# Causal attention and a squared-ReLU MLP on one core: product times v merged with the next pair's scores, and earlier ranks for the raw weights of the h stages

## The chip, the cores and the metric

The kernel runs on one core of a Trainium2 chip. The metric is the device time of one execution in microseconds (us), taken as the median over runs. Every engine (PE for matrix products, DVE, ACT and POOL for elementwise work, SP for issuing DMAs) works through its own instruction stream in order, and semaphores connect them.

## The reference, cut to what matters

```python
# q, k, v: (4, 12, 448, 64) float32; w_in: (768, 2048), w_out: (2048, 768), both float64
scores = (q @ k.T) / 8                        # per batch and head
scores = where(upper triangle, -1e9, scores)  # causal
attn = exp(scores - max); attn = attn / (sum + 1e-9)
x = (attn @ v) -> (1792, 768)                 # tokens by 12 heads * 64
h = maximum(x @ w_in, 0)
out = (h * h) @ w_out                         # (1792, 768) float32
```

## The kernel before

**Units of work.** Two heads of a batch form a pair: 24 pairs, numbered n = 0 to 23 in the code. Pairs 0 to 11 (batches 0 and 1) run at the start with two sets of buffers (`a` for even, `b` for odd n) and leave x in SBUF, split into two float32r parts. Pairs 13 to 24 of the count (n = 12 to 23) run later, one after the other in the order of the list `turns`, all in buffer set `a`, between the MLP matmuls of the first 896 tokens. Their results go to DRAM through `spill`, for the last part of the kernel.

**A pair** (function `attention`). The loads of q and k and every third time of v; two 32x32-block transposes on DVE; the scores (line 386: 28 float32 matmuls of 64x64 tiles for the seven chunks of 64 queries; n < 12 has them in two groups, n >= 12 in one); per chunk a mask-and-minimum on DVE (399) and an exp on ACT (403); the inverse of the sums (470, 471); seven normalisations on POOL or DVE (412); sixteen 128x128 transposes on PE in four banks (426), each bank copied to `pt` on ACT or DVE (434 or the helper at 311); then the product with v (446: 16 float32 matmuls with a 128x64 stationary tile) into one bank `av`; then x or the spill. In the spill of n >= 18 a DVE subtraction (513) reads `av` too.

**MLP.** The first 896 tokens go through four groups of 512 columns of d_ff. A group has an h stage (`h_unit`, lines 634 to 636: w_hi x_hi + w_hi x_lo + w_lo x_hi, six inner tiles, 448 columns) and an o stage (`o_unit`, 1010 to 1012, 384 columns). Its weights come as float64 words: `piece` loads 128 rows into one of three `raw` buffers (587), two ACT operations and three DVE operations (595, the helper at 314, 598) make float32 of them, and two more split it into float32r parts (helpers at 318 and 324). Six pieces of kind "i" serve an h stage, eight of kind "o" an o stage. The other 896 tokens go through seven products in place of eight (`h_pair`, `o_seven`), after about 398 us.

**What sets the order.** Nothing runs where it is written: `Plan.op` collects operations with a rank, what they read and write, and the time that they are reckoned to take; `Plan.emit` then puts them on the engines one at a time. Of all ready operations it takes the one that can start first by its own reckoning, and among equals the one of lower rank. An operation is one indivisible stretch of an engine's stream. `lag` delays the time from which it may be placed. A bank of PSUM is held through `Hold("ps", kind)`: eight banks, and for each kind a cap on how many are held at once (`mm` for MLP results, `sc` for scores, `pt` for transposes, `av`).

The ranks are written as times in us. Pair n < 12 has rank 8.6 n, and its q and k loads 14 less. The late pairs are spread evenly over the ranks of the four groups. A piece has a rank `at`; its load stands at `at - 12`, its ACT operations at `at - 4`, its DVE operations at `at - 2`, its split at `at`. For the first h stage `begin` is 10.0 and the other end is `start`, 12 * 8.6 + 4 = 107.2; for the later ones the two ends are those of the o stage before it.

```python
key = (w[1], o.rank)                              # start by the plan, then rank
groups = (ORDER[:3], ORDER[3:]) if n < NA else (ORDER,)
at = begin + (rank - begin) * (c + 0.5) / NP      # rank of piece c of an h stage
```

Of the kernel before, what the change touches and what calls it, by code (L numbers as in the profile page):

```python
# [9 lines left out]
F32 = mybir.dt.float32  # L10
# [7 lines left out]
PE, ACT, DVE, POOL, DMA, DMA2 = range(6)  # L18
# [147 lines left out]
def t_dve(n, fast=False):  # L166
    return n / 1920 + 0.15 if fast else n / 960 + 0.15
# [13 lines left out]
def t_dma(count, size):  # L181
    return count * (0.0084 + size * 0.0000488) / 16
# [3 lines left out]
def kernel(  # L186
# [21 lines left out]
    P = 128  # L208
# [3 lines left out]
    NP = H // 2  # L212
# [15 lines left out]
    CW = [QC * (c + 1) for c in range(NQ)]  # L228
# [4 lines left out]
    TURNED = [(c, kc) for kc in range(NK) for c in range(2 * kc, NQ)]  # L233
    TOFF = [P * next(i for i, t in enumerate(TURNED) if t[1] == kc) for kc in range(NK)]
    NV = 3
    NA = 2 * NP
# [4 lines left out]
    CB = NP // 2  # L241
# [17 lines left out]
    psum = ctx.enter_context(tc.tile_pool(name="psum", bufs=1, space=bass.MemoryType.PSUM))  # L259
    plan = Plan()  # L260

    def tiles(nm, n, shape, dtype, pool=const):
        return [pool.tile(shape, dtype, name=f"{nm}{i}") for i in range(n)]
# [18 lines left out]
    spare = [whole[:, i * S:(i + 1) * S].bitcast(F32) for i in range((2 * NRAW + NZ + NB) * PCW // S)]  # L282
# [10 lines left out]
        nc.gpsimd.memset(t[KLAST:, NK - 1], 0.0)  # L293
    plan.pool("v", v_t)
    plan.pool("mx", tiles("mx", 8, [P, 1], F32))
    plan.pool("ps", tiles("ps", 8, [P, 512], F32, psum), mm=2, sc=4, pt=2, av=1, st=5, os=7)

    make_identity(nc, ident[:, :P])
    nc.vector.tensor_copy(ident[:, P:], ident[:, :QC])
# [10 lines left out]
    def on_act(n, dst, src, psum=False, func=AF.Copy, more=0, **kw):  # L310
        return (ACT, t_act(n, psum, more), lambda: nc.scalar.activation(dst(), src(), func, **kw))  # L311

    def on_dve(n, dst, a, b, op, more=0.0):
        return (DVE, t_dve(n) + more, lambda: nc.vector.tensor_tensor(out=dst(), in0=a(), in1=b(), op=op))  # L314
# [17 lines left out]
                list(reads) + [(key, 0)], [(key, 1)], after, drop=drop)  # L332


    vs = {}

    def attention(s, n, at):

        b, hp = divmod(n, NP)
        nm = s.nm  # L340
        spare = (lambda us: us) if n >= NA else (lambda us: 0.0)
# [31 lines left out]
        def softmax(chunks, at):  # L373

            pss = {b: Hold("ps", "sc") for b in sorted({PLACE[c][0] for c in chunks})}

            def place(c):
                b, o = PLACE[c]
                return pss[b].t[:, o:o + CW[c]]

            def scores():
                for c in chunks:
                    for j in range(2):
                        mine = slice(j * D, (j + 1) * D)
                        h = j ^ (PLACE[c][0] & 1)
                        nc.tensor.matmul(  # L386
                            place(c)[h * QC:(h + 1) * QC], s.qt[mine, c * QC:(c + 1) * QC],
                            s.kt[mine, :CW[c]], start=True, stop=True, skip_group_check=True)
            holds = tuple(pss.values())
            plan.op(at, [(PE, 0.16 + sum(2 * CW[c] / 2400 + 0.01 for c in chunks), scores)],  # L390
                    [(nm, "qt"), (nm, "kt")], holds, take=holds,
                    clear=[(nm, "p", c) for c in chunks], lag=spare(0.6))
            for c in chunks:
                exponential(c, lambda c=c: place(c), pss[PLACE[c][0]], Hold("mx", "mx"), at)

# [41 lines left out]
        def times_v(av, at):  # L437

            first = 2 * (n % NV)

            def go():
                for kc in range(NK):
                    m = NQ - 2 * kc
                    p = s.pt[:, TOFF[kc]:TOFF[kc] + m * P].rearrange("p (c j i) -> p c j i", j=2, i=QC)
                    for j in range(2):
                        nc.tensor.matmul(  # L446
                            av.t[j * D:(j + 1) * D, kc * P:S], vr.t[:, kc, first + j], p[:, :, j],
                            start=kc == 0, stop=kc == NK - 1, skip_group_check=True,
                        )
            plan.op(at, [(PE, 0.2 + 4 * sum((S - kc * P) / 2400 for kc in range(NK)), go)],  # L450
                    [vr] + [(nm, "pt", i) for i in range(len(TURNED) // 4)], [av], take=av, drop=[vr],
                    lag=spare(1.0))

        for j in range(2):
            load_qk("k", k, s.k, j)
# [4 lines left out]
        vr = vs[n // NV]  # L460
# [13 lines left out]
        for c in range(NQ):  # L474
            normalise(c, keys, at)
        at += 2
        av = Hold("ps", "av")
        for i in range(len(TURNED) // 4):
            transposed_p(i, at)
        times_v(av, at + 1)  # L480
# [1 line left out]
        if n < NA:  # L482
            x = x_t[n]
            plan.op(at, [on_act(S, lambda: x[:, 0], lambda: av.t[:, :S], True)],
                    [av], [(("x", n), 0)])
            plan.op(at, [on_dve(S, lambda: x[:, 1], lambda: av.t[:, :S],
                                lambda: x[:, 0].bitcast(F32), ALU.subtract)],
                    [av, (("x", n), 0)], [(("x", n), 1)], drop=[av])
        else:
            spill(n - NA, av, at)  # L490

    xt_dram = nc.dram_tensor("xt_dram", (4, CB, P, S), F32, kind="Internal").ap()
# [2 lines left out]
    def spill(n, av, at):  # L495

        b, c = divmod(n, NP)
        gate, mark = list(last_sums), len(plan.ops)

        def result():  # L500
            return av.t[:, :S]

        def stored(h, place, key):
            plan.op(at, [(DMA, 0.5, lambda: nc.sync.dma_start(out=place, in_=h.t), t_dma(P, 4 * S))], [h], [key], drop=[h])

        def loaded(place, key):
            h = Hold("r", "xs")
            plan.op(at - 8, [(DMA, 0.5, lambda: nc.sync.dma_start(out=h.t, in_=place), t_dma(P, 4 * S))],
                    [key], [h], gate, take=h)
            return h  # L510

        def less(h, drop):
            plan.op(at, [(DVE, t_dve(S) + 0.05, lambda: nc.vector.tensor_tensor(
                out=h.t, in0=result(), in1=h.t, op=ALU.subtract))], [av], [h], drop=drop)

        def t_place(k):
            return xt_dram[k - 1, c % CB], ("xt", k, c % CB)
        second = b == 1
        if second and c < CB:
            h = loaded(x_dram[c], ("xd", c))  # L520
            less(h, [av])
            stored(h, *t_place(1))
        elif second:
            t1 = loaded(*t_place(1))
            x21 = loaded(x_dram[c], ("xd", c))
            x12 = loaded(x_dram[n - CB], ("xd", n - CB))
            less(t1, [av])
            plan.op(at, two_sources(S, lambda: x21.t, lambda: x21.t, lambda: t1.t, ALU.subtract),
                    [t1], [x21])
            plan.op(at, [(DVE, t_dve(S) + 0.05, lambda: nc.vector.tensor_tensor(  # L530
                out=x12.t, in0=x12.t, in1=result(), op=ALU.subtract))], [av], [x12], drop=[av])
            stored(t1, *t_place(2))
            stored(x12, *t_place(3))
            stored(x21, *t_place(4))
        xs = Hold("r", "xs")
        plan.op(at, [
            on_act(S, lambda: xs.t, result, True),
            (DVE, t_dve(S) + 0.05, lambda: nc.vector.tensor_copy(xs.t, result())),
        ], [av], [xs], take=xs, drop=[av])
        last_sums[:] = plan.ops[mark:]  # L540
        stored(xs, x_dram[n], ("xd", n))
# [507 lines left out]
    def group(gr, rank, step, begin):  # L1049

        for c in range(NP):
            at = begin + (rank - begin) * (c + 0.5) / NP
            piece(at, "i", gr, c, 0, ())
            if gr in (0, NG - 1):
                keep(at + 4, gr, c, swap)
        begin = rank
        if gr == 0:
            r = NP * PAIR + 16
            for f in range(GF):
                r = h_unit(f, 0, r, (start - r) / (GF - f) / NP)  # L1060
            for f in range(GF):
                rank = h_unit(f, 1, rank, H_US * step)
        else:
            for f in range(GF):
                for h in range(2):
                    rank = h_unit(f, h, rank, H_US * step)
        for i in range(2 * GF):
            at = begin + (rank - begin) * (i + 0.5) / 8
            piece(at, "o", gr, i % GF, i // GF, swap)
        begin = rank  # L1070
        for ch in range(2):
            for t in range(NT):
                rank = o_unit(gr, t, ch, rank, O_US * step, swap)
        return begin, rank

    rank, begin = start, 10.0
    rest = NG * (2 * GF * NP * H_US + 2 * NT * GF * O_US) - GF * NP * H_US
    for gr in range(NG):
        begin, rank = group(gr, rank, (rest + NA * 7.0) / rest, begin)
    mark = len(plan.ops)  # L1080
    turns = [NA + NP * b + CB * g + i for g in range(2) for b in range(2) for i in range(CB)]
    for i, n in enumerate(turns):
        attention(even, n, start + i * (rank - start - 42) / NA)

# [32 lines left out]
    for gr, u in stages:  # L1117
        last = gr == TURNS[-1]
        if u is None:
            W = o_parts(gr, rank - LEAD, rank + 42 * H_US - LEAD)  # L1120
            rank = o_last(W, rank, H_US) if last else o_seven(gr, W, rank, H_US)
        else:
            W = w_parts(gr, u, rank - LEAD, rank + 7 * CB * H_US - LEAD)
            rank = h_pair(gr, u, W, rank, H_US, last)
# [33 lines left out]
```

## Time and profile before

| | |
|---|---|
| median of 3 runs | 616.55 us (613.45 to 618.95) |
| the profiled execution: its own time | 616.22 us |
| its span in the trace | 614.5 us |
| busy share of the span | PE 96%, PE weight loads 83%, DVE 71%, ACT 58%, POOL 57% |
| mean granted PE clock | 0.994 of full speed |
| DMA | 120.01 MB, mean 195 GB/s |

The span is what the trace covers; the execution's own time has 1.7 us around it. The views used below are the page's busy times, busy times by stretch, waits by engine, the order of instructions in time, and the chain of work that ended last. In the order of instructions, columns are start, busy time from first start to last end, engine, line, operation, tiles, shape and count; matmuls overlap, so the time that one takes of PE is the distance from its start to the next start.

### The profile page before, as it was taken

The numbers are of one execution on the slowest core, as the hardware profiler recorded it, in microseconds if no ns is written. First come the engines' busy times: TensorE is split into PE (matmuls) and PEld (weight loads), VectorE is DVE, ScalarE is ACT, GpSimd is POOL, SyncE is SP. The second block draws the span as 40 slices with busy tenths as digits, with TensorE's granted clock in tenths as the row PEclk, the third lists the DMA queues.
The fourth block names the chain that finished last, engine by engine and source line by source line (L and its number), as shares of the span: only waits on it lengthen the run. The fifth ranks groups of instructions, "written<-read, shape, count | busy, mean of one in ns | idle before, by whom it ended". The sixth has DMA issues, their size and how long they took to land.

```text
span 614.5 us, 11390 instructions
## 1 busy us (share of the span) xinstructions
PE 589.3 (96%) x3714; PEld 511.0 (83%) x3714; DVE 436.9 (71%) x957; ACT 356.7 (58%) x878; POOL 352.5 (57%) x460
## 2 busy tenths in 40 slices
PE   3888999999999999999999999999999999999996
PEld 1555677789988988988998889989989999998995
DVE  4888776366786689785787326679994896399474
ACT  3787998657677845678555552247665534661220
POOL 2556575475589746788644764325865674478110
PEclk9899999999999999999999999999999999999999
DMA  9788856597888999998997477877958837963546
GB/s 140 159 199 146 175 99 132 106 308 243 249 222 256 293 264 220 275 265 277 245 279 249 163 209 220 266 219 194 228 103 198 224 71 161 221 105 95 149 76 106
DMA packets 203148, 120.01 MB, mean 195 GB/s; under 512 B 138960, under 2 KB 191056, under 8 KB 203088
## 3 DMA queue, kind: packets, MB, share of 16 engines
q1 hardware_dynamic: 181328, 108.01, 64.4%
q0 software_dynamic: 6912, 9.44, 10.2%
q10 hardware_dynamic: 14848, 1.84, 2.0%
q8 instruction: 29, 0.48, 0.3%
q14 instruction: 31, 0.25, 0.1%
HBM read 80.71 MB, written 38.54 MB: 194 GB/s over the span
## 4 chain that ended last, share of the span: by engine, by line
PE 81%; DVE 8%; DMA 5%; ACT 3%; issue 1%; POOL 1%; SPq 1%; DVEq 0%; ACTq 0%; POOLq 0%
PE ps L1010 7%; PE ps L634 7%; PE ps L1012 6%; PE ps L1011 6%; PE ps L636 6%; PE ps L635 6%; PE ps L426 6%; PE ps L446 6%; PE ps L386 5%; PE ps L937 5%; PE ps L939 5%; PE ps L938 5%; PE ps L815 4%; PE ps L811 4%; PE ps L813 4%; DVE g L314 2%
## 5 line engine op out<-in xcount | busy, mean ns | idle before, releaser
L412 POOL TENSOR_SCALAR ap<-ap,asm 128x128 f32<-128x128 f32 (+6 forms) x122 | 72.7, 615 | 52.3 <-DVE asm L471 41.6
L311 ACT ACTIVATE words<-words 128x384 f32<-128x384 f32 (+3 forms) x135 | 77.3, 596 | 32.9 <-DVE words L314 9.7
L399 DVE CUSTOM_DVE_ANT_0 ps<-ps,mask 128x448 f32<-128x448 f32 (+6 forms) x168 | 68.7, 444 | 28.2 <-PE ps L386 22.8
L1010 PE MATMUL ps<-wo,g 128*128 128x384 f32 x224 | 77.0, 344 | 0.0
L634 PE MATMUL ps<-x,wi 128*128 128x448 f32 x192 | 75.0, 391 | 0.6 <-ACT x L311 0.6
L1012 PE MATMUL ps<-wo,g 128*128 128x384 f32 x224 | 75.1, 335 | 0.0
L1011 PE MATMUL ps<-wo,g 128*128 128x384 f32 x224 | 75.0, 335 | 0.0
L636 PE MATMUL ps<-x,wi 128*128 128x448 f32 x192 | 70.9, 369 | 0.4 <-DVE wi L314 0.4
L635 PE MATMUL ps<-x,wi 128*128 128x448 f32 x192 | 70.7, 368 | 0.2 <-DVE x L314 0.2
L403 ACT ACTIVATE ap<-ps,mx 128x448 f32<-128x448 f32 (+6 forms) x126 | 58.7, 482 | 13.5 <-DVE mx L399 12.5
L937 PE MATMUL ps<-g,wi 128*128 128x448 f32 x162 | 59.5, 367 | 1.0 <-DVE sb L314 0.9
L311 ACT ACTIVATE r<-ps 128x448 f32<-128x448 f32 x59 | 32.1, 545 | 48.3 <-PE ps L815 15.8
L938 PE MATMUL ps<-g,wi 128*128 128x448 f32 x162 | 59.3, 366 | 0.0
L318 POOL TENSOR_TENSOR wi<-words,wi 128x384 fp32r<-128x384 f32 (+1 forms) x45 | 56.3, 1263 | 5.1 <-ACT wi L311 2.4
L939 PE MATMUL ps<-g,wi 128*128 128x448 f32 x162 | 59.2, 366 | 0.0
L324 POOL TENSOR_SCALAR wi<-words 128x384 fp32r<-128x384 f32 (+1 forms) x40 | 26.8, 672 | 47.4 <-DVE words L598 14.4
L811 PE MATMUL ps<-x,wi 128*128 128x448 f32 x141 | 51.8, 368 | 0.0
L813 PE MATMUL ps<-x,wi 128*128 128x448 f32 x141 | 51.7, 367 | 0.0
L815 PE MATMUL ps<-x,wi 128*128 128x448 f32 x141 | 51.7, 366 | 0.0
L314 DVE CUSTOM_DVE_ANT_0 words<-words 128x768 uint16<-128x768 uint16 (+1 forms) x56 | 45.7, 816 | 5.3 <-ACT words L311 1.9
L311 ACT ACTIVATE apt<-ps 128x512 f32<-128x512 f32 x70 | 38.4, 602 | 17.4 <-PE ps L426 17.4
L595 DVE TENSOR_SCALAR words<-words 128x384 int32<-128x384 int32 (+1 forms) x56 | 29.1, 521 | 21.5 <-ACT words L311 21.1
(138 smaller groups left out, 1476.1 us busy)
## 6 DMA issues: line engine op xcount, KB each, us to landing
words<-in_moe_w_in_dram SPq DMA_DIRECT2D x24, 512.0 KB, 5.3
words<-in_moe_w_out_dram SPq DMA_DIRECT2D x32, 384.0 KB, 4.2
wo_split<-wo SPq DMA_DIRECT2D x26, 384.0 KB, 4.8
wi<-wo_split SPq DMA_DIRECT2D x24, 384.0 KB, 4.5
wo_whole<-words SPq DMA_DIRECT2D x32, 192.0 KB, 4.0
wi_split<-wi SPq DMA_DIRECT2D x24, 256.0 KB, 4.0
v<-in_v_dram SPq DMA_DIRECT2D x24, 192.0 KB, 4.2
wi_whole<-words SPq DMA_DIRECT2D x18, 256.0 KB, 4.3
```

The costliest lines, as they stand in the source:

```text
L311: return (ACT, t_act(n, psum, more), lambda: nc.scalar.activation(dst(), src(), func, **kw))
L634: nc.tensor.matmul(o, w[:, 0], x[:, 0], start=c == 0, stop=False)
L635: nc.tensor.matmul(o, w[:, 0], x[:, 1], start=False, stop=False)
L636: nc.tensor.matmul(o, w[:, 1], x[:, 0], start=False, stop=c == NP - 1)
L811: nc.tensor.matmul(o, w.t[:, 0, c], x[:, 0], start=begin and c == 0, stop=False, skip_group_check=True)
L813: nc.tensor.matmul(o, w.t[:, 0, c], x[:, 1], start=False, stop=False, skip_group_check=True)
L937: nc.tensor.matmul(o, w.t[:, 0, d], g.t[:, 0], start=start, stop=False, skip_group_check=True)
L938: nc.tensor.matmul(o, w.t[:, 0, d], g.t[:, 1], start=False, stop=False, skip_group_check=True)
L939: nc.tensor.matmul(o, w.t[:, 1, d], g.t[:, 0], start=False, stop=stop, skip_group_check=True)
L1010: nc.tensor.matmul(res(), g[:, 0], w[:, 0], start=f == 0, stop=False)
L1011: nc.tensor.matmul(res(), g[:, 0], w[:, 1], start=False, stop=False)
L1012: nc.tensor.matmul(res(), g[:, 1], w[:, 0], start=False, stop=f == GF - 1)
```

## The change

The product with v of a late pair is no longer an operation of its own. For all late pairs but the last it is put on a list (`waiting`) with its bank, its reads, the hold on v and its spill; the next pair's scores operation takes it up: it issues the 16 product matmuls first and then its own 28 score matmuls, reads what both read, and takes five banks at once (four for scores, one for `av`, now of kind `sc`, whose cap goes from 4 to 5). The spill of the earlier pair is entered after it, at the rank of the next pair's scores plus 2. The lag of the joint operation is that of the scores, 0.6, where the product alone had 1.0. The last late pair keeps its own product and spill.

The second edit multiplies the span over which the six pieces of an h stage are ranked by 0.9, in all four groups, from the same beginning.

```diff
-    plan.pool("ps", tiles("ps", 8, [P, 512], F32, psum), mm=2, sc=4, pt=2, av=1, st=5, os=7)
+    plan.pool("ps", tiles("ps", 8, [P, 512], F32, psum), mm=2, sc=5, pt=2, av=1, st=5, os=7)
...
-    vs = {}
+    vs, waiting = {}, []
+    turns = [NA + NP * b + CB * g + i for g in range(2) for b in range(2) for i in range(CB)]
...
             def scores():
+                if before:
+                    before[0][1]()
                 for c in chunks:
...
-            holds = tuple(pss.values())
-            plan.op(at, [(PE, 0.16 + sum(2 * CW[c] / 2400 + 0.01 for c in chunks), scores)],
-                    [(nm, "qt"), (nm, "kt")], holds, take=holds,
+            holds, before = tuple(pss.values()), list(waiting)
+            waiting.clear()
+            more = [x for w in before for x in w[2]]
+            avs = tuple(w[0] for w in before)
+            plan.op(at, [(PE, 0.16 + 1.9 * len(before) + sum(2 * CW[c] / 2400 + 0.01 for c in chunks), scores)],
+                    [(nm, "qt"), (nm, "kt")] + more, holds + avs, take=holds + avs, drop=[w[3] for w in before],
                     clear=[(nm, "p", c) for c in chunks], lag=spare(0.6))
+            for w in before:
+                w[4](at + 2)
...
+            reads = [vr] + [(nm, "pt", i) for i in range(len(TURNED) // 4)]
+            if n in turns[:-1]:
+                waiting.append((av, go, reads, vr, lambda rank: spill(n - NA, av, rank)))
+                return
             plan.op(at, [(PE, 0.2 + 4 * sum((S - kc * P) / 2400 for kc in range(NK)), go)],
-                    [vr] + [(nm, "pt", i) for i in range(len(TURNED) // 4)], [av], take=av, drop=[vr],
-                    lag=spare(1.0))
+                    reads, [av], take=av, drop=[vr], lag=spare(1.0))
...
-        av = Hold("ps", "av")
+        av = Hold("ps", "sc" if n in turns[:-1] else "av")
...
-        else:
+        elif n == turns[-1]:
             spill(n - NA, av, at)
...
-            at = begin + (rank - begin) * (c + 0.5) / NP
+            at = begin + 0.9 * (rank - begin) * (c + 0.5) / NP
```

## Rows read from the trace of the kernel before

**Rows 1.** The page, busy time, share of the span and instructions by engine:
```profile
PE 589.3 (96%) x3714; PEld 511.0 (83%) x3714; DVE 436.9 (71%) x957; ACT 356.7 (58%) x878; POOL 352.5 (57%) x460
```
**Rows 2.** Busy times by stretch; the first line names the columns:
```profile
core 0: us, PE busy (x) PEld busy (x) DVE busy (x) ACT busy (x) POOL busy (x), PEclk, DMA share, GB/s
...
31.00:65.00 34.00, 28.95 (x259) 19.53 (x253) 27.57 (x87) 27.21 (x81) 18.97 (x31) 0.95 0.86 181
65.00:120.00 55.00, 53.90 (x464) 39.75 (x457) 38.16 (x130) 44.94 (x139) 31.00 (x55) 1.00 0.58 111
120.00:398.00 278.00, 278.00 (x1832) 247.41 (x1831) 190.33 (x422) 166.95 (x406) 182.67 (x216) 1.00 0.87 250
398.00:614.50 216.50, 210.08 (x1028) 192.14 (x1026) 161.25 (x244) 100.70 (x203) 107.89 (x128) 1.00 0.67 155
```
**Rows 3.** Order of PE's instructions, 152 to 159 us, separate operations:
```profile
152.18 0.34 PE L1012 MATMUL ps<-wo,g 128*128 128x384 f32 x1
152.44 1.95 PE L446 MATMUL ps<-apt,v 128*64 128x448 f32 x16
154.32 0.44 PE L1010 MATMUL ps<-wo,g 128*128 128x384 f32 x1
154.61 0.34 PE L1011 MATMUL ps<-wo,g 128*128 128x384 f32 x1
154.78 0.34 PE L1012 MATMUL ps<-wo,g 128*128 128x384 f32 x1
...
156.34 0.34 PE L1012 MATMUL ps<-wo,g 128*128 128x384 f32 x1
156.61 1.75 PE L386 MATMUL ps<-akt,aqt 64*64 64x448 f32 x28
158.29 0.44 PE L1010 MATMUL ps<-wo,g 128*128 128x384 f32 x1
158.57 0.34 PE L1011 MATMUL ps<-wo,g 128*128 128x384 f32 x1
```
**Rows 4.** Order of PE's instructions, 176 to 181 us, adjacent operations:
```profile
176.07 0.36 PE L636 MATMUL ps<-x,wi 128*128 128x448 f32 x1
176.36 1.95 PE L446 MATMUL ps<-apt,v 128*64 128x448 f32 x16
178.24 1.75 PE L386 MATMUL ps<-akt,aqt 64*64 64x448 f32 x28
179.92 0.47 PE L634 MATMUL ps<-x,wi 128*128 128x448 f32 x1
180.23 0.36 PE L635 MATMUL ps<-x,wi 128*128 128x448 f32 x1
180.43 0.36 PE L636 MATMUL ps<-x,wi 128*128 128x448 f32 x1
```
**Rows 5.** The chain that ended last, the other adjacent place (start, us):
```profile
283.41 1.88 PE ps L446 x16
285.29 1.66 PE ps L386 x20
```
**Rows 6.** Order of ACT's instructions, copies of transposes for the pair of rows 3:
```profile
149.54 1.09 ACT L311 ACTIVATE apt<-ps 128x512 f32<-128x512 f32 x2
```
**Rows 7.** PE's waits, 31 to 65 us (total, times, longest us):
```profile
PE ps L426 <- ACT ap L403: 2.5, 1, 2.5
PE ps L386 <- ACT bpt L311: 1.0, 1, 1.0
```
**Rows 8.** Order of ACT's instructions, 44 to 60 us (idle before, releaser):
```profile
44.28 0.68 ACT L311 ACTIVATE words<-words 128x512 f32<-128x512 f32 x1 [1.71 <-DMA words<-in_moe_w_in_dram]
...
59.20 1.22 ACT L311 ACTIVATE words<-words 128x512 f32<-128x512 f32 x2 [3.09 <-DMA words<-in_moe_w_in_dram]
```
**Rows 9.** Order of PE's instructions, scores at 45 us:
```profile
45.49 2.80 PE L386 MATMUL ps<-bkt,bqt 64*64 64x448 f32 x28 [1.02 <-ACT bpt L311]
```
**Rows 10.** PE's waits, 398 us to the end (total, times, longest us):
```profile
PE ps L937 <- DVE sb L314: 0.9, 1, 0.9
```

## The prediction before the run

> **What bounds the kernel now.** I read the page's busy times first: PE is busy 589.3 us of a 614.5 us span [rows 1], so at most some 25 us can come from PE waiting less; all else has to come from PE doing less or doing it faster. The busy times by stretch say where those 25 us lie [rows 2]. From 120 to 398 us, where all late pairs run, PE is busy for the whole 278.00 us at full clock: no wait there can be shortened, and only time that PE's own stream takes counts. After 398 us it is idle for 216.50 - 210.08 = 6.4 us; one wait of 0.9 us on DVE is the only one listed [rows 10], the rest is the tail after the last matmul. From 65 to 120 us it is idle for 1.1 us. From 31 to 65 us it is idle for 34.00 - 28.95 = 5.05 us and the granted clock is 0.95, not 1.00. What is left of the 25.2 us, 12.6 us, lies in the first 31 us. So the first edit has to be priced in a stretch bound by PE, and the second in the stretch from 31 to 65 us, the only one in which the order of weights meets idle PE.
>
> **The joined operation, PE's own time.** The order of PE's instructions shows what a burst of float32 matmuls costs beside its own matmuls. In the o stage one MLP matmul follows the other at 0.17 us (154.61 to 154.78). The last one before the product with v takes 152.18 to 152.44, 0.26 us; the first one after it takes 154.32 to 154.61, 0.29 us. The scores are the same: 156.34 to 156.61 is 0.27 us on the way in, 158.29 to 158.57 is 0.28 us on the way out [rows 3]. So going in costs 0.09 to 0.10 us and coming out 0.11 to 0.12 us, some 0.20 us for each excursion. The bursts take 154.32 - 152.44 = 1.88 us and 158.29 - 156.61 = 1.68 us. In one place the plan before already put the two side by side: the product takes 178.24 - 176.36 = 1.88 us, the scores 179.92 - 178.24 = 1.68 us, with one entry (0.29 against 0.20 us for an h matmul, 180.23 to 180.43) and one exit (0.31 us) for both [rows 4]. The joint therefore costs nothing that a start-to-start distance shows, and a merge saves one entry and one exit: 0.20 us.
>
> Eleven products are merged. Two already stand next to their scores [rows 4, 5] and save nothing. In the nine others MLP matmuls stand between, as in rows 3. That is 9 x 0.20 = 1.8 us, in a stretch with no PE idle time to swallow it. Bounds: nothing, if the plan scatters its transposes into as many more excursions, and 11 x 0.23 = 2.5 us.
>
> A rule speaks against the full amount. The Trainium skill, page "TensorEngine Tiling (Array Packing)", section "Tiling Modes", says that a change of tiling mode drains the engine. Product and scores have different tile shapes, so by that rule the joint would still pay one change, three in place of four, and an estimate by it is half of the saving, 0.9 us. Rows 4 speak for the full 1.8 us: a drain at the joint would have made one of the two bursts longer than when it stands alone.
>
> **The joined operation, what it waits for.** It now waits for the last pair's four copies of transposes as well as for q and k. In rows 3 the copies that ACT makes run from 149.54 us for 1.09 us [rows 6], so they end near 150.6 us; the joint operation would start where the scores now end less both bursts, 158.29 - 1.68 - 1.88 = 154.7 us. That is 4 us of cover, and the scores themselves end where they did. In the two adjacent places it starts where the product started before. I cost this wait at nothing; if the cover went, MLP matmuls queued behind on PE would wait, by some tenths of a us for each pair. The five banks: four are free because the last pair's exps are long done (its transposes could not have run otherwise), and the fifth because the spill of the pair before that is a whole pair older. PSUM adds no wait.
>
> **The spill.** It moves from just after the product to just after the next scores, in rows 3 some 2 us, elsewhere up to the distance between a product and the next scores. It issues one store for each pair and for the six pairs with n >= 18 loads and stores more, on SP's queue; the same number as before, all behind loads that have been there longer. Nothing before 398 us reads what it stores, except later spills a pair or more away. The last pair, whose end lets the last part's x tiles be loaded, keeps its own product and spill. The DVE subtraction waits in DVE's order for the joint operation as it did for the product; the next pair's masking stands ahead of it by rank. Cost: nothing, covered by a pair's length (178.24 to 156.61, 21.6 us) [rows 3, 4].
>
> **The weights of the late h stages.** Three of the four sixes are ordered while PE has no idle time [rows 2], so earlier pieces buy nothing there. They cost nothing either as long as PE stays full.
>
> **The weights of the first h stage.** The six ranks run from 18.1 to 99.1 before and from 17.3 to 90.2 after (10 + 97.2 (c + 0.5) / 6, with 0.9 on the second term). The piece c = 1 has its load moved from 22.3 to 19.9, past the loads of pair 4 (4 x 8.6 - 14 = 20.4), and c = 2 from 38.5 to 34.5, past those of pair 6 (37.6); the last two move by 7 and 9. In this stretch ACT stood in front of a conversion whose words had not landed, for 1.71 us and for 3.09 us [rows 8], with exps queued behind it; PE waited 2.5 us for an exp and 1.0 us behind a copy of ACT's [rows 7]. PE also loses speed: after the wait of 1.02 us the scores took 2.80 us against 1.75 us of the same burst at full clock [rows 9, 3], 1.05 us more. A clock of 0.95 over 34 us is 1.7 us of lost PE time [rows 2]. So the most that this edit can gain is 5.05 + 1.7 = 6.75 us. Its loss is bounded by the nearest event: one more landing wait of the longest kind, 3.09 us, and the slow scores behind it, 1.05 us, together 4.1 us. Between -6.75 and +4.1 us I take -1.0 us: weights that are ready earlier let PE place matmuls of the h stage in the 2.5 us wait, and the two products of one inner tile on two open banks are six matmuls of 0.20 us, 1.2 us; but the ACT and DVE work pulled forward is work in front of exps.
>
> **The sum.** -1.8 - 1.0 = -2.8 us on the profiled execution's 616.22 us (span 614.5 and 1.7 around it) gives 613.4 us. The median shown, 616.55 us, is 0.3 us higher, which gives 613.7; I say 613.5 us.
>
> **The rivals.**
> - Much of the idle time of the first stretch goes. For it: ACT's two landing waits are an accident of order, and order is what changes. Against: the loads remain the same and the DMA engines are 0.86 busy there [rows 2]. Half of 6.75 us and the merge give 616.2 - 3.4 - 1.8 = 611.0 us, all of it 607.7 us.
> - Slower: a conversion moved ahead of exps meets words that have not landed. Place: ACT's stream between 31 and 65 us. Price: 4.1 us for each event like the second of rows 8, less the merge's 1.8: 618.5 us for one, 622.6 us for two. It decides as soon as ACT reaches a piece's first conversion before its load lands with exps behind it that PE needs next, which is what rows 7 and 8 show once. For it: it has happened; against: loads move earlier along with conversions.
> - The merge doesn't save what it says, because the plan spends the freed time on extra excursions, or because the last part gives it back on its waits: 616.2 - 0 to 1.0 = 615 to 616.5 us. For it: after 398 us PE does have a wait on DVE [rows 10]. Against: DVE's work there starts from PE's results, so it moves along.
> - The joint drains as in the tiling rule: 0.9 + 1.0 gives 614.3 us. This lies within the forecast's own range.
>
> **How the numbers follow.** Forecast (612 to 615 us, the tiling rule's 614.3 within it, a tenth by itself): 0.50. Much of the idle time gone (607.7 to 612): 0.20. Nothing saved (615 to 617): 0.15. Slower (617 to 623 and a little over): 0.15. The range 609.5 to 618.0 us leaves out about 0.08 below and 0.10 above. What a measurement of this kernel can tell from no change is 1%, 6.2 us: faster means under 610.4 us, which only the better half of the first rival reaches, 0.14; slower means over 622.7 us, two landing waits or more, 0.06; the same, 0.80.
>
> **What the profile after would show.** The merge: eleven bursts of line 446 followed at once by line 386 between 120 and 398 us, no PE wait in that stretch, and MLP matmuls as many as before; the stretch from the first late scores to the end of the o stages shorter by about 1.8 us. The weights: PE idle and the clock between 31 and 65 us against 5.05 us and 0.95, and ACT's waits for words against 1.71 and 3.09 us. The forecast is wrong if a PE wait appears in front of a joint operation, if the joint shows a longer burst than 1.88 + 1.68 us, or if the first 120 us move by more than 3 us either way.

## The result: 0.55% slower, and the profile after

The changed kernel took 620.71 us (median of 16 runs, 618.47 to 624.32) against 618.25 us (16 runs, 613.45 to 620.77): ratio 1.0055, 95% interval 1.003 to 1.0079. The forecast was 613.5 us with a range up to 618.0. Of the runs of before that the forecast started from, the profiled one (616.22 us) lies 2 us below the median of all; the profiled execution of after (618.50 us) likewise. TensorE's granted clock, as the mean over a run, was 0.984 to 0.996 of full speed in the sixteen runs of after and 0.996 in the profiled one, so its trace shows the changed kernel at its best.

Busy times of after by stretch, columns as in [rows 2]:

```profile
31.00:65.00 34.00, 28.32 (x238) 18.57 (x236) 26.54 (x87) 26.39 (x80) 17.22 (x28) 0.95 0.78 161
65.00:120.00 55.00, 54.17 (x464) 40.70 (x459) 40.28 (x135) 45.70 (x139) 31.22 (x53) 1.00 0.59 120
120.00:398.00 278.00, 277.29 (x1834) 248.22 (x1834) 193.76 (x428) 168.67 (x407) 181.53 (x215) 1.00 0.88 252
398.00:616.70 218.70, 209.28 (x1021) 190.78 (x1019) 161.50 (x236) 102.02 (x204) 112.53 (x131) 1.00 0.65 151
```

Up to 398 us little has changed. After it PE is idle for 218.70 - 209.28 = 9.4 us where it was 6.4 us [rows 2]. The first matmul of the seven products starts at 396.75 us (398.04 before) and the last matmul of all at 611.12 us (608.77 before): the profiled execution was 1.3 us ahead when the last part began and 2.3 us behind when it ended.

The joint operation itself is what the rows of before said. Order of PE's instructions of after, 153 to 157 us (lines 454 and 389 are now the product with v and the scores):

```profile
153.06 0.34 PE L1023 MATMUL ps<-wo,g 128*128 128x384 f32 x1
153.33 1.95 PE L454 MATMUL ps<-apt,v 128*64 128x448 f32 x16
155.21 1.75 PE L389 MATMUL ps<-akt,aqt 64*64 64x448 f32 x28
156.89 0.44 PE L1021 MATMUL ps<-wo,g 128*128 128x384 f32 x1
157.17 0.34 PE L1022 MATMUL ps<-wo,g 128*128 128x384 f32 x1
```

One entry (0.27 us), 1.88 us, 1.68 us, one exit (0.28 us), against two of each in [rows 3]. No PE wait stands in front of any of the eleven joint operations. The waits of PE between 120 and 398 us are these two (total, times, longest), both elsewhere:

```profile
PE ps L1023 <- POOL g L318: 0.4, 1, 0.4
PE ps L434 <- POOL ap L420: 0.3, 1, 0.3
```

PE's waits from 396 us to the end, which answer to [rows 10]:

```profile
PE ps L948 <- DVE sb L314: 3.1, 2, 1.7
PE ps L822 <- DMA w<-wi_split: 0.6, 1, 0.6
PE ps L948 <- DVE sa L314: 0.5, 1, 0.5
```

The 0.9 us has become 3.1 us. The DVE additions that PE waits for (`sb`, a sum that empties a bank) stand behind one held subtraction; "held" means here that the profile shows an instruction as busy for far longer than others of its shape. DVE of after, in order of time:

```profile
549.01 1.50 DVE L314 TENSOR_TENSOR g<-r,g 128x448 fp32r<-128x448 f32 x1
550.43 5.85 DVE L314 TENSOR_TENSOR g<-f,g 128x448 fp32r<-128x448 f32 x1
556.20 0.61 DVE L314 TENSOR_TENSOR sb<-ps,sb 128x448 f32<-128x448 f32 x1
```

POOL of after in the same time:

```profile
550.59 1.30 POOL L318 TENSOR_TENSOR wi<-words,wi 128x384 fp32r<-128x384 f32 x1
551.58 0.84 POOL L324 TENSOR_SCALAR g<-r 128x448 fp32r<-128x448 f32 x1
552.11 1.28 POOL L318 TENSOR_TENSOR wi<-words,wi 128x384 fp32r<-128x384 f32 x1
553.10 1.26 POOL L318 TENSOR_TENSOR w<-words,w 128x384 fp32r<-128x384 f32 x1
554.07 1.26 POOL L318 TENSOR_TENSOR wi<-words,wi 128x384 fp32r<-128x384 f32 x1
555.06 0.74 POOL L324 TENSOR_SCALAR wi<-words 128x384 fp32r<-128x384 f32 x1
```

And PE, which resumes twice after it (in brackets: idle before, releaser):

```profile
556.87 0.47 PE L948 MATMUL ps<-g,wi 128*128 128x448 f32 x1 [1.38 <-DVE sb L314]
...
560.08 0.47 PE L948 MATMUL ps<-g,wi 128*128 128x448 f32 x1 [1.73 <-DVE sb L314]
```

A subtraction that takes 0.61 us elsewhere lasted 5.85 us: it began beside the first of six POOL instructions without a gap and ended at 556.28 us, 0.48 us after the last of them (555.06 + 0.74 = 555.80). In the kernel before, POOL had nothing to do in these microseconds (3.02 us of idle ahead of its copy) and the DVE subtraction before it ran at full speed. POOL, then DVE, of the kernel before:

```profile
553.33 0.97 POOL L324 TENSOR_SCALAR g<-r 128x448 fp32r<-128x448 f32 x1 [3.02 <-ACT r L311]
```

```profile
552.19 0.61 DVE L314 TENSOR_TENSOR g<-f,g 128x448 fp32r<-128x448 f32 x1
```

Holds as such are not new. The kernel before has one of 4.26 us a little later, beside three POOL additions in a row (563.39 to 567.04 us); no PE wait stands behind it [rows 10]:

```profile
563.20 4.26 DVE L314 TENSOR_TENSOR wi<-f,wi 128x384 fp32r<-128x384 f32 x1
```

Neither edit touches this code. Its order comes from the same plan: of the 1131 operations entered for the last part, 90 stand on another engine than before, and the order differs on every engine (counted in the two plans). Theory A was therefore that the edits do save time and that the plan's new order of the last part loses more; the rivals, that the merge (B) or the earlier weights (C) cost by themselves.

### The profile page after: what moved, and what is told of

Same layout as the page of the kernel before. It is cut to its first block, busy times and chain, and to the rows that moved or that the text cites. A ratio compares the mean times of both kernels' runs of the same rounds, so it can differ in the third digit from the quotient of the medians.

```text
span 616.7 us, 11388 instructions
## 1 busy us (share of the span) xinstructions
PE 588.2 (95%) x3714; PEld 510.6 (83%) x3714; DVE 441.7 (72%) x956; ACT 360.9 (59%) x882; POOL 354.6 (58%) x457
## 4 chain that ended last, share of the span: by engine, by line
PE 81%; DVE 6%; DMA 4%; ACT 3%; POOL 2%; issue 1%; SPq 1%; DVEq 0%; POOLq 0%; ACTq 0%
PE ps L1021 6%; PE ps L645 6%; PE ps L1023 6%; PE ps L1022 6%; PE ps L647 6%; PE ps L646 6%; PE ps L454 5%; PE ps L822 5%; PE ps L824 5%; PE ps L826 5%; PE ps L434 5%; PE ps L948 5%; PE ps L950 5%; PE ps L949 5%; PE ps L389 4%; DVE g L314 2%
## 5 line engine op out<-in xcount | busy, mean ns | idle before, releaser
L420 POOL TENSOR_SCALAR ap<-ap,asm 128x64 f32<-128x64 f32 (+6 forms) x122 | 74.9, 635 | 52.4 <-DVE asm L482 35.7
L311 ACT ACTIVATE words<-words 128x384 f32<-128x384 f32 (+3 forms) x130 | 75.1, 597 | 35.0 <-DVE words L314 11.8
L645 PE MATMUL ps<-x,wi 128*128 128x448 f32 x192 | 73.9, 385 | 0.0
L647 PE MATMUL ps<-x,wi 128*128 128x448 f32 x192 | 70.3, 366 | 0.4 <-DVE wi L314 0.4
L646 PE MATMUL ps<-x,wi 128*128 128x448 f32 x192 | 70.2, 366 | 0.0
L318 POOL TENSOR_TENSOR wi<-words,wi 128x384 fp32r<-128x384 f32 (+1 forms) x46 | 59.8, 1311 | 6.3 <-ACT wi L311 4.8
L948 PE MATMUL ps<-g,wi 128*128 128x448 f32 x153 | 56.2, 367 | 3.6 <-DVE sb L314 3.1
L824 PE MATMUL ps<-x,wi 128*128 128x448 f32 x153 | 56.2, 368 | 0.0
L822 PE MATMUL ps<-x,wi 128*128 128x448 f32 x153 | 56.1, 367 | 0.0
L826 PE MATMUL ps<-x,wi 128*128 128x448 f32 x153 | 56.0, 366 | 0.0
L949 PE MATMUL ps<-g,wi 128*128 128x448 f32 x153 | 55.9, 365 | 0.0
L950 PE MATMUL ps<-g,wi 128*128 128x448 f32 x153 | 55.9, 365 | 0.0
L314 DVE CUSTOM_DVE_ANT_0 words<-words 128x768 uint16<-128x768 uint16 (+1 forms) x56 | 41.3, 738 | 9.3 <-ACT words L311 6.5
L314 DVE TENSOR_TENSOR g<-r,g 128x448 fp32r<-128x448 f32 x43 | 35.6, 845 | 13.6 <-POOL g L324 10.7
```

The source lines that it names most:

```text
L645: nc.tensor.matmul(o, w[:, 0], x[:, 0], start=c == 0, stop=False)
L646: nc.tensor.matmul(o, w[:, 0], x[:, 1], start=False, stop=False)
L647: nc.tensor.matmul(o, w[:, 1], x[:, 0], start=False, stop=c == NP - 1)
L822: nc.tensor.matmul(o, w.t[:, 0, c], x[:, 0], start=begin and c == 0, stop=False, skip_group_check=True)
L824: nc.tensor.matmul(o, w.t[:, 0, c], x[:, 1], start=False, stop=False, skip_group_check=True)
L826: nc.tensor.matmul(o, w.t[:, 1, c], x[:, 0], start=False, stop=c == CB - 1, skip_group_check=True)
```

## The experiments

All ratios are against the kernel before on the same chip at the same time, with 95% intervals. "Stretch" is the time from the first matmul of the seven products to the last matmul of all; it is 210.7 us in the kernel before and 214.4 us in the changed one.

**Each edit alone.** E1 takes the second edit back, E2 makes it alone:

```diff
 E1, in the changed kernel:
-            at = begin + 0.9 * (rank - begin) * (c + 0.5) / NP
+            at = begin + (rank - begin) * (c + 0.5) / NP
 E2, in the kernel before:
-            at = begin + (rank - begin) * (c + 0.5) / NP
+            at = begin + 0.9 * (rank - begin) * (c + 0.5) / NP
```

> The changed kernel without the second edit: products with v are merged, the pieces of the h stages keep their old ranks. Theory A (the last part): the two edits save time up to about 398 us, and the loss lies after it, because the plan's order there came out differently and puts DVE work behind POOL work; from about 540 us on this kernel has the changed kernel's order. A expects the stretch from the first seven-product matmul to the end of the span at 219 to 220 us (216.5 before, 220.0 in the changed kernel), PE waits of 3 to 4 us in all near 550 us, and a time 1 to 3 us over that of the kernel before. Theory B (the first edit costs by itself): PE waits in front of joint operations between 120 and 398 us, that stretch longer than before by 2 us or more. Theory C (the second edit costs by itself): this kernel is 1.5 to 2 us faster than before.

Measured: 623.61 us (6 runs), ratio 1.0083 (1.0052 to 1.0113); 618.38 us x 0.0083 = 5.1 us, above the 1 to 3 that A had named. That it is slower than both edits together is not shown: the intervals overlap. Stretch 216.2 us. E1's plan of the last part is a third one, but near 550 us it has the changed kernel's order: the held subtraction is there again, and PE's waits behind it. DVE of E1, and PE's waits from 540 us on:

```profile
551.09 5.86 DVE L314 TENSOR_TENSOR g<-f,g 128x448 fp32r<-128x448 f32 x1
```

```profile
PE ps L948 <- DVE sb L314: 3.1, 2, 1.7
```

> The kernel before with the second edit alone (factor 0.9). Its plan has the same order as the kernel before on every engine from the first seven-product operation on. Theory A (the last part): no loss; 216 to 217 us from the first seven-product matmul to the end, a time 0 to 3 us below that of the kernel before. Theory B (the merge costs by itself): the same as A here. Theory C (the earlier weights cost by itself): slower than before by 2 us or more, with PE waits in the first 120 us or in the h stages.

Measured: 617.41 us, ratio 0.9986 (0.9963 to 1.0009), stretch 211.9 us. E2's plan has the old order of the last part on every engine, and the second edit shows no loss; C falls. B is still open.

**Both kernels with the other's last part.** A list of the operations that a kernel planned from a certain point of its last part on (about 180 us; 915 and 903 of the 1131 operations), each with its engine, is written into the other kernel, and its plan has to follow it there:

```diff
+TAIL = [...]   # operation * 4 + way, in the order in which the other plan chose them
...
+        fixed, done = {id(self.ops[self.tail + x // 4]): x for x in TAIL}, 0
...
             for o in ready:
+                x = fixed.get(id(o))
+                if x is not None and x != TAIL[done]:
+                    continue
...
-                    for i, w in enumerate(o.ways)
+                    for i, w in enumerate(o.ways) if x is None or i == x % 4
...
+            done = min(done + (id(o) in fixed), len(TAIL) - 1)
```

> The changed kernel with both edits, but all operations that the kernel before plans for its last 180 us or so are forced into the order and onto the engines that the kernel before gives them. Theory A (the last part): the PE waits near 550 us fall from some 3.1 us to about 0.9 us as before, the last part takes 216 to 217.5 us, and the time is 2 to 4 us below the changed kernel, 0 to 2 us below the kernel before. Theories B and C (an edit costs by itself in the first 398 us): the same time as the changed kernel within 1 us.

Measured: 615.43 us, ratio 0.9959 (0.9938 to 0.9981), stretch 211.1 us; at 2.5 us under the kernel before a little more than A had named. PE's waits from 540 us on:

```profile
PE ps L1005 <- DVE sb L371: 0.9, 1, 0.9
```

> The kernel before without either edit, but all operations that the changed kernel plans for its last 180 us or so are forced into the order and onto the engines that the changed kernel gives them. Theory A (the last part): one DVE operation is held for 3 us or more beside consecutive POOL work near 550 us, PE waits there rise to 3 to 4 us, and the time is 2 to 4 us over that of the kernel before, though nothing of the change is in the kernel. Theories B and C: the time of the kernel before within 1 us.

Measured: 622.39 us, ratio 1.0065 (1.0043 to 1.0087), stretch 217.3 us. A kernel without either edit shows the loss and its sign in the trace. DVE, and PE's waits from 540 us on:

```profile
555.13 5.87 DVE L371 TENSOR_TENSOR g<-f,g 128x448 fp32r<-128x448 f32 x1
```

```profile
PE ps L994 <- DVE sb L371: 3.1, 2, 1.7
```

The two settle where the loss comes from: the order of the last part makes the changed kernel slower or faster than before, with the same edits ahead of it. The stretch is 210.7 to 211.9 us in the traces with the old order (before, E2, E3 and E7 below) and 214.4 to 217.3 us in those with the new order near 550 us (after, E5 below, E1, E4). Of these 2.5 to 6.6 us, the two waits behind the held subtraction are 2.2 us (3.1 - 0.9) in every one of the four.

A second part comes with it in three of the four, and in no trace with the old order (from 398 us to the last matmul): around the second of PE's two idle times (1.4 and 1.7 us) TensorE's granted clock falls to 0.50, its level of 1.2 GHz, for 3.41 us in E4 (565.12 to 568.53 us) and in E5, and for 6.83 us in E1. From 555 to 570 us, columns as in [rows 2], of after, E1, E4 and E5:

```profile
555.00:570.00 15.00, 11.90 (x58) 10.37 (x57) 13.58 (x24) 1.09 (x3) 6.57 (x8) 1.00 0.28 79
555.00:570.00 15.00, 11.90 (x45) 10.19 (x44) 12.88 (x21) 1.87 (x4) 6.14 (x9) 0.77 0.15 24
555.00:570.00 15.00, 11.90 (x50) 10.21 (x49) 14.68 (x18) 3.74 (x8) 6.56 (x9) 0.89 0.09 13
555.00:570.00 15.00, 11.89 (x50) 10.16 (x49) 13.49 (x22) 1.80 (x4) 6.25 (x8) 0.89 0.18 44
```

In the same busy time PE gets through 58 matmuls at full clock, 50 and 45 at the lower means. A mean of 0.89 over 15 us is 1.7 us of lost PE time, 0.77 is 3.4 us, a part of it while PE waited. In after the same two waits left the clock at 1.00; how often the untraced runs lose it is not known. The rest is mostly shorter waits between 405 and 462 us, which vary from run to run (0.3 us in E1, 2.1 us in E4).

**Hold or load.** The changed kernel once more, for comparison on the same chip:

> The changed kernel once more, unchanged, so that the others of this call have it beside them on the same chip. Expected 1.004 to 1.008 of the kernel before; near 550 us one DVE subtraction of some 5.9 us and PE waits of some 3.1 us.

Measured: 620.95 us, ratio 1.0055 (1.0021 to 1.0088), a subtraction of 5.88 us, stretch 216.8 us.

E6 keeps the changed kernel's order of the last part by the same kind of list, but four of the POOL subtractions go to DVE:

```diff
-                      [h], w, gate, [h] if last else [], take=w, ways=OWAY)
+                      [h], w, gate, [h] if last else [], take=w, ways=HWAY if gr == 2 else OWAY)
+TAIL = [...]   # the changed kernel's own; the splits s2 and s4 of both halves on DVE, the others on POOL
```

> The changed kernel with its own order of the last 180 us, but four of the float32r splits of the o weights (the subtractions wi<-words,wi and w<-words,w that POOL runs one after the other from about 550 to 555 us) are done by DVE instead, at their places in the order. DVE gets 4 x 0.55 = 2.2 us more work just where PE waits for it. Theory A1 (DVE is held up by POOL's consecutive work, not by its own load): the longest subtraction near 550 us falls from 5.9 to under 2 us, PE waits for sb there fall from 3.1 to under 1.5 us, and the time is 1 to 3 us below the changed kernel. Rival A2 (DVE simply has too much work there, and the order is late by that): PE waits rise by about 2 us and the time is 1 to 2.5 us over the changed kernel.

Measured: 616.83 us, ratio 0.9986 (0.9963 to 1.0009), 4.1 us below the changed kernel's median on the same chip, more than A1 named; stretch 213.6 us, with 2.4 us of other waits between 405 and 456 us and the granted clock at 1.00 throughout. DVE of E6, the same subtraction and the first of the four moved ones:

```profile
548.82 1.50 DVE L371 TENSOR_TENSOR g<-f,g 128x448 fp32r<-128x448 f32 x1
550.25 0.55 DVE L371 TENSOR_TENSOR wi<-words,wi 128x384 fp32r<-128x384 f32 x1
```

PE's waits of E6 from 540 us on:

```profile
PE ps L1005 <- DVE sb L371: 0.4, 1, 0.4
PE ps L879 <- ACT r L368: 0.4, 1, 0.4
```

More work on the engine that PE waits for made the kernel faster, so it was not DVE's load (A2) but the time for which POOL kept it from working (A1).

**The merge by itself.** E7 is E1 with the old order of the last part, by E3's list:

> The first edit alone (products merged, old ranks of the weights), with the last 180 us or so in the order and on the engines of the kernel before. It prices the merge by itself. If a merge saves one entry and one exit as the rows of the kernel before show (9 x 0.20 us): 1.8 us below the kernel before, ratio 0.997. Theory B (the joint operation or the later spill costs by itself): the time of the kernel before or up to 3 us more, with PE waits in front of joint operations.

Measured: 616.93 us, ratio 0.9985 (0.9963 to 1.0007), stretch 210.8 us; 618.15 us x 0.0015 = 0.9 us saved (from 2.3 saved to 0.4 lost). The forecast's 1.8 us lies inside, and so does nothing; B's cost does not show. Its one longer PE wait between 120 and 398 us (1.7 us in E1) is not in front of a joint operation:

```profile
PE ps L1080 <- POOL g L375: 1.6, 1, 1.6
```

**Two attempts at the plan.** E8 makes the plan treat POOL's one-source copies as it treats its two-source work, which may not overlap DVE's two-source work in the plan. E9 lets the plan choose the engine of the splits that were bound to POOL:

```diff
 E8:
-            dst(), src(), 1.0, 1.0, op0=ALU.mult, op1=ALU.mult))
+            dst(), src(), 1.0, 1.0, op0=ALU.mult, op1=ALU.mult)) + SHARED
 E9:
-    HWAY, OWAY, GWAY = slice(None), slice(1, 2), slice(0, 1)
+    HWAY, OWAY, GWAY = slice(None), slice(None), slice(0, 1)
```

> The changed kernel in which the plan also treats POOL's one-source copies (the splits' first parts) as work that may not overlap DVE's two-source work, everywhere. In the held stretch near 550 us such copies stood in the gaps between POOL's subtractions. If the plan's blind spot is those copies, DVE subtractions of over 3 us disappear after 398 us and the time falls 1 to 4 us below the changed kernel. If real overlap comes from the plan drifting away from the chip (rival), holds of over 3 us remain somewhere and the time is that of the changed kernel or above, since the plan spends time on avoiding an overlap.

Measured: 617.49 us, ratio 0.9992 (0.9977 to 1.0008). The time fell by about as much as the first branch said, but a hold of over 3 us is there, as the rival said; PE does not wait behind this one:

```profile
549.05 4.23 DVE L314 TENSOR_TENSOR r<-r,f 128x448 f32<-128x448 f32 x1
```

POOL ran three subtractions in a row beside it and no copy, so the copies are not needed for a hold. Whether the gain has to do with the copies stays open, as the whole order is another.

> The changed kernel in which the float32r splits of the o weights of the last part may go to DVE or POOL as the plan sees fit, where they were bound to POOL. If POOL's consecutive subtractions are the hold, fewer of them in a row: PE waits near 550 us under 1.5 us and 1 to 4 us below the changed kernel. If the plan still puts them side by side on the chip, the time stays at the changed kernel's.

Measured: 615.43 us, ratio 0.9958 (0.9936 to 0.9981), stretch 211.5 us. It beats both kernels with one changed word, by more than the 1 to 4 us under the changed kernel that were expected (0.9958 against 1.0055). The whole order of the last part is another, so how much of the gain comes from the missing hold near 550 us is not shown. PE's only listed wait from 398 us on is another one:

```profile
PE ps L822 <- DMA w<-wi_split: 1.7, 1, 1.7
```

## Why the prediction was wrong

**The bound of the late pairs, and the price of a merge: right.** PE stayed nearly full there (0.7 us idle, the 0.4 and 0.3 us waits shown above), the joint operations show the bursts and the single entry and exit that [rows 3, 4] gave, and nothing waits in front of them. By itself the merge measured 0.9 us in E7 against 1.8 us forecast, with an interval that holds both and nothing too. E2 and E3 price it more closely: both have the early weights and the old last part, and up to the seven products they differ by the merge alone. From the first late scores to the first matmul of the seven products, E2, then E3:

```profile
110.84:398.02 287.18, 286.54 (x1896) 252.97 (x1895) 196.31 (x448) 173.40 (x424) 181.25 (x218) 1.00 0.86 246
112.36:397.32 284.96, 284.45 (x1895) 253.72 (x1895) 197.97 (x446) 173.63 (x424) 182.71 (x218) 1.00 0.87 248
```

With as many matmuls of each kind the merged one is 2.2 us shorter, and the medians differ by 617.41 - 615.43 = 2.0 us. In E2 no product stands next to its scores, so eleven joints are new there: 11 x 0.20 = 2.2 us.

**The tiling rule: no cost of it shows.** In the Trainium skill, page "TensorEngine Tiling (Array Packing)", section "Tiling Modes", a change of mode drains the engine. The trace shows no time lost to that at the joint: the joint of after shows 1.88 and 1.68 us from start to start, the durations of the bursts alone.

**The weights of the first h stage: near in size, not shown in mechanism.** The forecast took 1.0 us; E2 measured 618.38 us x 0.0014 = 0.9 us (2.3 saved to 0.6 lost). An interval that holds nothing as well makes the agreement at best luck. And the waits that were to be filled are still there. ACT's conversions of after between 44 and 60 us wait for their words as before:

```profile
44.74 0.66 ACT L311 ACTIVATE words<-words 128x512 f32<-128x512 f32 x1 [3.09 <-DMA words<-in_moe_w_in_dram]
...
59.43 1.21 ACT L311 ACTIVATE words<-words 128x512 f32<-128x512 f32 x2 [2.95 <-DMA words<-in_moe_w_in_dram]
```

That is 6.0 us against 4.8 us in [rows 8]. Over the whole stretch from 31 to 65 us the two kernels are alike; [rows 8] leave out a third wait of before, near 32 us. ACT's waits there, before, then after:

```profile
ACT words L311 <- DMA words<-in_moe_w_in_dram: 5.9, 3, 3.1
ACT words L311 <- DMA words<-in_moe_w_in_dram: 6.0, 2, 3.1
```

PE is idle for 5.7 us there (5.05 before). The slower rival had named such a wait and is not what happened either: the first 120 us of E3 and of the changed kernel come from the same edits, and E3 is faster than before.

**The sum as far as it went: right.** Both edits with the old last part (E3) measure 618.38 us x 0.0041 = 2.5 us saved (1.2 to 3.8); the sum said 2.8 us.

**The step that failed** is the sentence under the third rival that what follows 398 us cannot turn: "DVE's work there starts from PE's results, so it moves along". It holds for a fixed order. Here the order is made anew by a greedy plan whenever any operation ahead of it takes another time or another bank, and the edits changed 90 engine assignments in a part that they do not mention. The sum had no term for it. The rival with the last part was bounded by the loss of the gain, 616.5 us, as if that part could only give back what it got; the runs put 618.15 us x 0.0055 = 3.4 us of loss for the whole against 2.5 us of gain without the new order, 5.9 us between two orders of the last part (4.0 us between before and E4). Rows that could have warned of it were in the trace of before: DVE is the engine that PE waits for after 398 us [rows 10], and the hold of 4.26 us at 563.20 us, shown above, has no PE wait behind it.

What stays open is why some POOL instructions in a row let a DVE subtraction through after one of them and others do not, why the granted clock fell behind the two waits in three traces and not in the fourth, and what in the merge tips the plan: E2 alone leaves the order of the last part as it was, E1 alone gives the new one near 550 us, so it is the merge, but whether through the joint operation's reckoned time, its banks or the moved spill was not tried.

## What to carry to other kernels

Where a planner or compiler orders the whole program, price an edit with the order behind it held fixed, and then ask separately how far a re-planned order can move the time: here by 4.0 to 5.9 us, against 2.5 us for the edits. Diff the order and the engine choices of the parts that the edit does not mention before believing any sum, and measure with the old order forced on them. A DVE operation that takes ten times its usual time beside gapless POOL work is a conflict, not a load; moving the POOL work onto the busy DVE can be the cure, as in E6. It costs only where another engine needs what stands behind it.

## What the runs showed of the hardware

A DVE subtraction with both operands in SBUF waited through six consecutive POOL instructions, 5.85 to 5.88 us in place of 0.61, in four traces (after, after again, E1, E4). DVE operations with one operand in PSUM were never held from 398 us on. The groups of DVE instructions of after from 396 us on, with busy time and mean ns of one:

```profile
L314 DVE TENSOR_TENSOR sb<-ps,sb 128x448 f32<-128x448 f32 x45 | 26.3, 610 | 9.0 <-PE ps L950 8.8
...
L314 DVE TENSOR_TENSOR g<-f,g 128x448 fp32r<-128x448 f32 x16 | 17.7, 1118 | 5.8 <-ACT g L311 5.8
```

The sums from PSUM keep 610 ns; these sixteen splits from SBUF, the held one among them, average 1118 ns. The Trainium skill, page "SBUF — State Buffer", section "Who interferes with whom", says that a DVE instruction with two SBUF inputs contends with a GpSimd instruction that reads SBUF, and that issue order decides who blocks. The traces agree that it blocks (5.85 us) and that the sums from PSUM are exempt (610 ns); they add that the block can outlast the POOL instruction that began it. Which of the two came first they leave open: the held subtraction is recorded 0.16 us ahead of POOL's first instruction. The block need not last as long as POOL has the next one ready: in the kernel before, a DVE split was through after 1.34 us beside four POOL subtractions in a row. POOL, then DVE:

```profile
554.27 4.31 POOL L318 TENSOR_TENSOR wi<-words,wi 128x384 fp32r<-128x384 f32 x4
555.39 1.34 DVE L314 TENSOR_TENSOR g<-r,g 128x448 fp32r<-128x448 f32 x1
```
